# Row maxima of an attention kernel: mask products taken out, one maximum per 64 keys, and a VectorE minimum with a constant table

## The chip, the cores and the metric

The kernel runs on one core of a Trainium2 chip. The metric is the time of one execution on the device in microseconds (us). The engines that matter are TensorE (PE in the profile; PEld are its weight loads), VectorE (DVE), ScalarE (ACT), GpSimd (POOL) and SyncE (SP), which issues nearly all DMAs.

## The reference, cut to what matters

Attention over blocks of 64 positions is followed by a soft mixture of experts and a feed-forward layer. The change concerns the first line on the maximum alone.

```python
# q, k, v: (8, 8, 576, 64); attention of one batch and head:
scores = scale * np.matmul(q, k.transpose(0, 1, 3, 2))
block_i, block_j = pos[:, None] // 64, pos[None, :] // 64
scores = np.where(block_i >= block_j, scores, -1000000000.0)
scores = scores - np.max(scores, axis=-1, keepdims=True)
attn = np.exp(scores)
attn = attn / (np.sum(attn, axis=-1, keepdims=True) + 1e-09)
out = np.matmul(attn, v)
# then, on x = out as (4608, 512): soft mixture of 8 experts, and relu(x @ w_in)**2 @ w_out
```

A query sees all keys of its own block of 64 and of those before it.

## The kernel before, in words

**Stages.** Attention takes the first 430 us or so, the experts come next, and the last third is the feed-forward layer, a dense run of products. The weights of the experts are loaded while attention still runs.

**Attention.** The 64 heads are worked on in 32 pairs: a pair holds one head in each half of a tile, and four pairs make a batch. `pair(n)` writes one turn of a software pipeline: scores and exponentials of pair `n`, values of pair `n - 1`, row maxima of pair `n + 2`, splitting and transposing of pair `n + 3`, and, once in four pairs, the logits and slot weights of a batch that is done (`batch`, whose parts are handed out as `work`). TensorE's order is fixed as it is written; the order of the other engines and of SP's queue is made by a scheduler from dependencies.

**Row maxima.** 576 positions are four units of 128 and a tail of 64. `maxpass(n)` multiplies query units (tile `t`, also called `t1`) by keys (tile `s`, `s1`) into PSUM tiles `ps_max` of 512 columns: `chunk(0)` to `chunk(4)` for the units, and `chunk(5)` and `chunk(6)` for the tails. Each 128 query rows hold two blocks of 64, so in the last 128 keys of a unit the upper 64 rows may not see the second 64 keys. A further product per chunk (`mask`, line 459) adds a huge negative number there: the column tile `mrow_r` of the constant 60000 against the row tile `mrow_l`, which is -60000 for rows 0 to 63 and zero below. VectorE then reduces 512 columns to 4 numbers, one for each 128 keys (`red`, line 465), into tile `pm`, 8 rows of 4 per partition, of which there are two in turn. `fin` reduces `pm` to the row maxima `mx` (lines 498, 499 and 502), writes them as two float16 numbers into tile `qb` (lines 504 and 507), and lets SP transpose `qb` into tile `t2`, also written `t<-qb` (line 512). The second product of `scores` (line 528) subtracts the maximum by means of `t2`.

**Around it on VectorE.** Line 419 makes the low parts of keys (`ka`) and queries (`qb`); `ka` is then transposed by a DMA into `s` (line 426). Lines 364 to 383 work out scales of a pair. Lines 184 to 202 decode the weights `tin`. Lines 761 to 785 are the running maximum of a batch's logits (`mxb`, `mb`, `mrun`, `nm`), and line 816 scales the tokens `x`. On GpSimd, line 571 adds exponentials (`ss`) and line 711 adds the logits of heads (`ul`, `lg`, `ltl`). GpSimd's additions read two tiles in SBUF, as VectorE's lines 507 and 772 do.

Of the kernel before, what the change touches and what calls it, by code (L numbers as in the profile page):

```python
# [8 lines left out]
F32 = mybir.dt.float32  # L9
F32R = mybir.dt.float32r  # L10
F16 = mybir.dt.float16
U32 = mybir.dt.uint32
AF = mybir.ActivationFunctionType
ALU = mybir.AluOpType
# [4 lines left out]
BIG = 60000.0  # L19
# [4 lines left out]
def tile_attn_soft_moe_ffn(  # L24
# [12 lines left out]
    nc = tc.nc  # L37
# [198 lines left out]
    def attention():  # L236
# [13 lines left out]
        mid = st_m.enter_context(tc.tile_pool(name="mid", bufs=1))  # L250
# [10 lines left out]
        NBQ = 3  # L261
        qb = [(even, mid, nat_p)[i].tile([128, NBLK, 128], F16, name=f"qb{i}") for i in range(NBQ)]
        s2 = [pers[i].tile([128, NBLK, 128], F16, name=f"s2_{i}") for i in range(NB2)]
        pm = [mid.tile([128, 8, 4], F32, name=f"pm{i}") for i in range(2)]
        mxs = [mid.tile([128, NBLK], F32, name=f"mx{i}") for i in range(2)]
        junk = mid.tile([128, NBLK, D], mybir.dt.float8e4, name="junk")
        id16 = mid.tile([128, 128], F16, name="id16")
        mrow_l = mid.tile([128, 128], F16, name="mrow_l")
        mrow_r = mid.tile([128, 2], F16, name="mrow_r")

        def prepare():
            nc.vector.tensor_copy(id16, ident)
            for t in qb:
                nc.vector.memset(t, 0.0)
                for i in range(2 * NU):
                    u = i // 2
                    nc.vector.memset(t[0:64, i:i + 1, 66 + u:67 + u], -BIG)
                for h in range(2):
                    nc.vector.memset(t[64 * h:64 * h + 64, 2 * NU:2 * NU + 1, 70 + h:71 + h], -BIG)
            for t in pm:  # L280
                nc.vector.memset(t, -3.0e38)
            nc.vector.memset(mrow_l, 0.0)
            nc.vector.memset(mrow_l[0:1, 0:64], -BIG)
            nc.vector.memset(mrow_r, BIG)
            hi = slice(64, 128)
            a = sm_p.tile([128, 7], F32, tag="sc_a", name="cst")
            nc.vector.tensor_tensor(out=a[hi, 6:7], in0=ident[hi, 64:65], in1=ident[hi, 65:66], op=ALU.add)
            nc.vector.scalar_tensor_tensor(
                out=a[hi, 0:6], in0=ident[hi, 66:72], scalar=BIG / SHIFT, in1=a[hi, 6:7].to_broadcast([64, 6]),
                op0=ALU.mult, op1=ALU.add,  # L290
            )
            for t in s2:
                def put(o, x):
                    nc.vector.tensor_scalar(out=o, in0=x, scalar1=SHIFT, scalar2=None, op0=ALU.mult)

                put(t[hi, 0:8, 0:64], a[hi, 6:7].unsqueeze(2).to_broadcast([64, 2 * NU, 64]))
                for h in range(2):
                    put(t[hi, 8, 64 * h:64 * h + 64], a[hi, 5 - h:6 - h].to_broadcast([64, 64]))
                    put(t[hi, h:8:2, 64:128], a[hi, 0:4].unsqueeze(2).to_broadcast([64, NU, 64]))
# [143 lines left out]
        def maxpass(n):  # L443
            t1, s1 = T[n][0], T[n][1]
            pmt = pm[n % 2]
# [1 line left out]
            ptl = sm_p.tile([128, 5], F32, tag="ptl", name="ptl")  # L447
            mx = mxs[n % 2]

            def part(ps, hp, u, c0):  # L450
                nc.tensor.matmul(  # L451
                    ps[:, c0:c0 + 128 * (u + 1)].rearrange("p (s c) -> p s c", c=128), t1[:, 2 * u + hp, :],
                    s1[:, hp:2 * u + 2:2, :], start=(c0 == 0), stop=False,
                )

            def mask(ps, c0, step, cnt):
                o = ps[:, 0:512].rearrange("p (a x) -> p a x", x=128)
                o = o[:, c0 // 128:c0 // 128 + (cnt - 1) * (step // 128) + 1:max(step // 128, 1), 64:128]
                nc.tensor.matmul(o, mrow_l, mrow_r[:, 0:1].to_broadcast([128, 64 * cnt]), start=False, stop=True)  # L459

            def red(ps, o, w, cnt=None):
                i = ps[:, 0:w].rearrange("p (a x) -> p a x", x=min(128, w))
                if cnt:
                    i = ps[:, 0:w].rearrange("p (c a x) -> p c a x", c=cnt, x=128)
                nc.vector.tensor_reduce(out=o, in_=i, axis=AX.X, op=ALU.max)  # L465

            def chunk(i):
                ps = ps_r.tile([128, 512], F32, tag="r", name="ps_max")
                if i < 2:
                    part(ps, i, 0, 0)  # L470
                    part(ps, i, 2, 128)
                    mask(ps, 0, 384, 2)
                    red(ps, pf[:, 8 * i + 3:8 * i + 7], 512)
                elif i == 2:
                    part(ps, 0, 1, 0)
                    part(ps, 1, 1, 256)
                    mask(ps, 128, 256, 2)
                    red(ps, pmt[:, 4:6, 0:2], 512, 2)
                elif i < 5:
                    part(ps, i - 3, 3, 0)  # L480
                    mask(ps, 384, 128, 1)
                    red(ps, pmt[:, 3 + i, :], 512)
                else:
                    for hp in range(2):
                        h0 = 64 * hp
                        nc.tensor.matmul(
                            ps[h0:h0 + 64, 0:512].rearrange("p (s c) -> p s c", c=128) if i == 5
                            else ps[h0:h0 + 64, 0:64],
                            t1[:, 8, h0:h0 + 64],
                            s1[:, hp:8:2, :] if i == 5 else s1[:, 8, h0:h0 + 64],  # L490
                            start=True, stop=True,
                        )
                    red(ps, ptl[:, 0:4] if i == 5 else ptl[:, 4:5], 512 if i == 5 else 64)

            def fin():
                mv = mx[:, 0:8].rearrange("p (u h) -> p h u", h=2)
                pv4 = pmt.rearrange("p (a b) c -> p a b c", b=2)
                nc.vector.tensor_reduce(out=mv[:, :, 0:3:2], in_=pv4[:, 0:2], axis=AX.X, op=ALU.max)
                nc.vector.tensor_reduce(
                    out=mv[:, :, 1:4:2].rearrange("p h u -> p u h"), in_=pv4[:, 2:4], axis=AX.X, op=ALU.max  # L500
                )
                nc.vector.tensor_reduce(out=mx[:, 8:9], in_=ptl, axis=AX.X, op=ALU.max)
                t = qb[n % NBQ]
                nc.vector.tensor_scalar(
                    out=t[:, :, 64:65], in0=mx.unsqueeze(2), scalar1=-1.0 / SHIFT, scalar2=None, op0=ALU.mult
                )
                nc.vector.scalar_tensor_tensor(
                    out=t[:, :, 65:66], in0=mx.unsqueeze(2), scalar=-1.0 / SHIFT, in1=t[:, :, 64:65],
                    op0=ALU.mult, op1=ALU.subtract,
                )  # L510
                t2 = (mid, odd)[n % 2].tile([128, NBLK, 128], F16, tag="t2", name="t2")
                nc.sync.dma_start_transpose(out=t2, in_=t.rearrange("p s c -> p (s c)"))
                T[n][2] = t2
# [1136 lines left out]
```

## Time and profile before

| what | value |
|---|---|
| median of 3 runs | 893.66 us (890.32 to 896.48) |
| the profiled execution's own time | 893.13 us |
| its span, first to last instruction | 891.3 us |
| TensorE busy | 827.2 us, 93% |
| VectorE busy | 692.7 us, 78% |
| ScalarE busy | 627.5 us, 70% |
| GpSimd busy | 248.3 us, 28% |

The shares are means over stages of different kinds. GpSimd works nearly only in attention. A matmul's busy time includes its way through the pipeline, so two matmuls overlap and a busy TensorE is not one at its peak.

### The profile page before, as it was taken

To read this page: it belongs to the slowest core of one execution; us is meant where nothing else is said; L and a number is where in the kernel's file an instruction comes from. 1 tells how busy PE (TensorE), PEld (TensorE's weight loads), DVE (VectorE), ACT (ScalarE), POOL (GpSimd) and SP (SyncE) were. 2 spreads that over 40 slices of the span, in tenths; PEclk is the share of its full clock that TensorE was granted. 3 is DMA by queue.
4 is the path that set the end of the run, shared out by engine and by line. 5 is a ranking of instruction groups with operands and counts; after the bars stand their busy time and mean duration, and the time that the engine had idled before them with its cause. 6 is when DMAs were issued, how large, how long until landed. Compare 5 with 4: busy or idle time off the path is not lost.

```text
span 891.3 us, 22010 instructions
## 1 busy us (share of the span) xinstructions
PE 827.2 (93%) x8788; PEld 612.9 (69%) x8788; DVE 692.7 (78%) x1600; ACT 627.5 (70%) x1012; POOL 248.3 (28%) x394
## 2 busy tenths in 40 slices
PE   2778999999999989979997799999999999999997
PEld 1446766676666757656532444799998998889996
DVE  5857789989999997953632899888778888888880
ACT  5478787777878786734212789987788888887770
POOL 0234647566665855563100000000000000000000
PEclk9889999999999999999998899999999999999999
DMA  8788899999997797496999500100010000000002
GB/s 168 151 167 159 163 202 174 199 189 198 174 194 157 172 168 172 96 254 194 319 371 371 224 0 1 49 25 25 34 39 25 25 24 25 25 25 24 25 25 48
DMA packets 225191, 113.18 MB, mean 127 GB/s; under 512 B 193856, under 2 KB 202048, under 8 KB 225088
## 3 DMA queue, kind: packets, MB, share of 16 engines
q1 hardware_dynamic: 222432, 111.12, 53.1%
q8 instruction: 69, 1.13, 0.5%
q10 hardware_dynamic: 2656, 0.66, 0.4%
q14 instruction: 34, 0.28, 0.1%
HBM read 78.71 MB, written 9.44 MB: 99 GB/s over the span
## 4 chain that ended last, share of the span: by engine, by line
PE 60%; DVE 9%; DMA 8%; POOL 8%; ACT 8%; SPq 4%; issue 3%; ACTq 0%; DVEq 0%
PE ps_y L1464 14%; PE ps_x L1464 9%; PE ps_z L1464 9%; PE xm L601 5%; POOL ss L571 4%; PE ps_hb L1428 3%; POOL ul L711 3%; DMA s<-ka 3%; PE ps_sc L528 3%; PE po L1486 2%; DMA s<-s 2%; DVE pm L465 2%; PE ps_h L1154 2%; PE ps_max L451 1%; PE tl L612 1%
## 5 line engine op out<-in xcount | busy, mean ns | idle before, releaser
L1464 PEld LDWEIGHTS <-ah 128*128 128x128 f16 x1792 | 170.5, 98 | 21.8 <-issue 0.2
L566 ACT ACTIVATE p<-ps_sc,es 128x512 f32<-128x512 f32 x192 | 128.0, 692 | 40.4 <-PE ps_sc L528 25.9
L1397 DVE TENSOR_TENSOR al<-a,ah 128x1024 f16<-128x1024 f32 (+1 forms) x128 | 138.8, 1127 | 16.9 <-ACT ah L1451 15.5
L571 POOL TENSOR_TENSOR ss<-p 128x384 f32<-128x384 f32 (+1 forms) x128 | 92.8, 746 | 172.7 <-ACT p L566 172.6
L465 DVE TENSOR_REDUCE pm<-ps_max 128x4 f32<-128x512 f32 x160 | 107.4, 683 | 32.1 <-PE ps_max L459 31.8
L1451 ACT CAST ah<-a 128x1024 f16<-128x1024 f32 (+1 forms) x128 | 114.4, 936 | 15.3 <-DVE a L1397 14.0
L528 PE MATMUL ps_sc<-t,s 128*128 128x512 f16 (+3 forms) x512 | 107.7, 304 | 11.4 <-DMA s<-s 7.1
L1557 POOL TENSOR_TENSOR ot<-u,p 128x256 f32<-128x256 f32 x16 | 12.4, 777 | 377.2 <-DVE u L1528 341.5
L1464 PE MATMUL ps_y<-bh,ah 128*128 128x256 f16 x384 | 104.8, 273 | 0.0
L1464 PE MATMUL ps_y<-bl,ah 128*128 128x256 f16 x384 | 104.7, 273 | 0.0
L1464 PE MATMUL ps_y<-bh,al 128*128 128x256 f16 x384 | 104.7, 273 | 0.0
L571 POOL TENSOR_TENSOR ss<-ss,p 128x320 f32<-128x320 f32 (+1 forms) x128 | 98.1, 766 | 10.6 <-ACT p L566 1.5
L1319 ACT ACTIVATE r<-ps_hb,alpha 128x1024 f32<-128x1024 f32 x64 | 71.1, 1112 | 33.9 <-PE ps_hb L1428 33.3
L1464 PEld LDWEIGHTS <-al 128*128 128x128 f16 x896 | 87.7, 98 | 10.0
L601 PE MATMUL xm<-p,ar_hi 128*64 128x256 f32 (+3 forms) x512 | 91.4, 456 | 0.0
L1397 DVE TENSOR_TENSOR a<-a 128x256 f32<-128x256 f32 x192 | 76.2, 425 | 3.9
L1464 PE MATMUL ps_x<-bh,ah 128*128 128x256 f16 x256 | 70.1, 274 | 0.0
L1464 PE MATMUL ps_z<-bh,ah 128*128 128x256 f16 x256 | 69.9, 273 | 0.0
L1464 PE MATMUL ps_x<-bh,al 128*128 128x256 f16 x256 | 69.8, 273 | 0.0
L1464 PE MATMUL ps_z<-bl,ah 128*128 128x256 f16 x256 | 69.8, 273 | 0.0
L1464 PE MATMUL ps_x<-bl,ah 128*128 128x256 f16 x256 | 69.8, 273 | 0.0
L1464 PE MATMUL ps_z<-bh,al 128*128 128x256 f16 x256 | 69.8, 273 | 0.0
(255 smaller groups left out, 1849.7 us busy)
## 6 DMA issues: line engine op xcount, KB each, us to landing
wch<-in_moe_w_dram SPq DMA_DIRECT2D x12, 1024.0 KB, 8.4
ar_hi<-in_v_dram SPq DMA_DIRECT2D x64, 128.0 KB, 3.3
raw<-in_moe_w_in_dram SPq DMA_DIRECT2D x16, 512.0 KB, 5.0
wch<-in_moe_w_dram SPq DMA_DIRECT2D x16, 512.0 KB, 9.0
out_dram<-ot SPq DMA_DIRECT2D x32, 256.0 KB, 2.1
ar_hi<-in_moe_w_dram SPq DMA_DIRECT2D x6, 1024.0 KB, 7.9
s<-s SPq DMA_DIRECT2D x32, 144.0 KB, 3.2
ar_lo<-in_k_dram SPq DMA_DIRECT2D x32, 128.0 KB, 3.1
```

Source lines behind the costliest of these rows:

```text
L465: nc.vector.tensor_reduce(out=o, in_=i, axis=AX.X, op=ALU.max)
L528: nc.tensor.matmul(ps[:, c0:c0 + w].rearrange("p (s c) -> p s c", c=128), kk[:, 2 * t + hp, :], qq[:, 2 * u0 + hp:8:2, :], start=(c0 == 0 ...
L566: exps[:] = [nc.scalar.activation(out=pt, in_=ps, func=AF.Exp, scale=es[:, 0:1])]
L571: add = lambda o, x, y: nc.gpsimd.tensor_tensor(out=o, in0=x, in1=y, op=ALU.add)
L601: nc.tensor.matmul(box["xm"][64 * hp:64 * hp + 64, 128 * t:512], vs[:, t, hp, :], r, start=(t == 0), stop=(t == 3),)
L711: add = lambda o, x, y: nc.gpsimd.tensor_tensor(out=o, in0=x, in1=y, op=ALU.add)
L1154: nc.tensor.matmul(hp_[fh][32 * e4:32 * e4 + 32, :], si[:, dt, s0:s0 + 32], wt[8 * g + KD * fh + dt][e4], start=(dt == 0), stop=(dt == KD ...
L1319: nc.scalar.activation(out=r[:, c0:c1], in_=ps[:, c0:c1], func=AF.Relu, **kw)
L1397: sub = lambda o, a, b: nc.vector.tensor_tensor(out=o, in0=a, in1=b, op=ALU.subtract)
L1428: nc.tensor.matmul(ps[:, 512 * j + 256 * a:512 * j + 256 * a + 256], ws[:, 128 * f:128 * f + 128], ctt[:, c0:c0 + 256], start=True, stop=True,
L1451: nc.scalar.copy(v(hl[n % 2][0][:, 2 * kq:2 * kq + 2], s), v(a7[n, kq], s))
L1464: nc.tensor.matmul(acc[:, 0:HM], a[:, k], b[:, k], start=bool(first and k + j == 0), stop=(k == KH - 1 and j == 2), skip_group_check=not f ...
```

## The change

The mask products and their two constant tiles go. The maximum is taken over 64 keys at a time, so that `red` gives 8 numbers for 512 columns where it gave 4, and `pm` has 8 rows of 8. The forbidden combinations are then single numbers in `pm`. A constant table `cap` (64 partitions of 64 numbers) holds -3e38 at those places and 3e38 elsewhere, and `fin` begins with one VectorE minimum of `pm`'s upper 64 partitions with `cap`, in place. The reductions behind it read 8 numbers where they read 4.

```diff
--- before.py
+++ after.py
@@ -261,12 +261,11 @@
         NBQ = 3
         qb = [(even, mid, nat_p)[i].tile([128, NBLK, 128], F16, name=f"qb{i}") for i in range(NBQ)]
         s2 = [pers[i].tile([128, NBLK, 128], F16, name=f"s2_{i}") for i in range(NB2)]
-        pm = [mid.tile([128, 8, 4], F32, name=f"pm{i}") for i in range(2)]
+        pm = [mid.tile([128, 8, 8], F32, name=f"pm{i}") for i in range(2)]
         mxs = [mid.tile([128, NBLK], F32, name=f"mx{i}") for i in range(2)]
         junk = mid.tile([128, NBLK, D], mybir.dt.float8e4, name="junk")
         id16 = mid.tile([128, 128], F16, name="id16")
-        mrow_l = mid.tile([128, 128], F16, name="mrow_l")
-        mrow_r = mid.tile([128, 2], F16, name="mrow_r")
+        cap = mid.tile([64, 64], F32, name="cap")
 
         def prepare():
             nc.vector.tensor_copy(id16, ident)
@@ -279,9 +278,9 @@
                     nc.vector.memset(t[64 * h:64 * h + 64, 2 * NU:2 * NU + 1, 70 + h:71 + h], -BIG)
             for t in pm:
                 nc.vector.memset(t, -3.0e38)
-            nc.vector.memset(mrow_l, 0.0)
-            nc.vector.memset(mrow_l[0:1, 0:64], -BIG)
-            nc.vector.memset(mrow_r, BIG)
+            nc.vector.memset(cap, 3.0e38)
+            for c0, c1, d in ((7, 24, 16), (13, 30, 16), (35, 44, 8), (55, 64, 8)):
+                nc.vector.memset(cap[:, c0:c1:d], -3.0e38)
             hi = slice(64, 128)
             a = sm_p.tile([128, 7], F32, tag="sc_a", name="cst")
             nc.vector.tensor_tensor(out=a[hi, 6:7], in0=ident[hi, 64:65], in1=ident[hi, 65:66], op=ALU.add)
@@ -447,39 +446,31 @@
             ptl = sm_p.tile([128, 5], F32, tag="ptl", name="ptl")
             mx = mxs[n % 2]
 
-            def part(ps, hp, u, c0):
+            def part(ps, hp, u, c0, last):
                 nc.tensor.matmul(
                     ps[:, c0:c0 + 128 * (u + 1)].rearrange("p (s c) -> p s c", c=128), t1[:, 2 * u + hp, :],
-                    s1[:, hp:2 * u + 2:2, :], start=(c0 == 0), stop=False,
-                )
-
-            def mask(ps, c0, step, cnt):
-                o = ps[:, 0:512].rearrange("p (a x) -> p a x", x=128)
-                o = o[:, c0 // 128:c0 // 128 + (cnt - 1) * (step // 128) + 1:max(step // 128, 1), 64:128]
-                nc.tensor.matmul(o, mrow_l, mrow_r[:, 0:1].to_broadcast([128, 64 * cnt]), start=False, stop=True)
-
-            def red(ps, o, w, cnt=None):
-                i = ps[:, 0:w].rearrange("p (a x) -> p a x", x=min(128, w))
+                    s1[:, hp:2 * u + 2:2, :], start=(c0 == 0), stop=last,
+                )
+
+            def red(ps, o, w, x, cnt=None):
+                i = ps[:, 0:w].rearrange("p (a x) -> p a x", x=x)
                 if cnt:
-                    i = ps[:, 0:w].rearrange("p (c a x) -> p c a x", c=cnt, x=128)
+                    i = ps[:, 0:w].rearrange("p (c a x) -> p c a x", c=cnt, x=x)
                 nc.vector.tensor_reduce(out=o, in_=i, axis=AX.X, op=ALU.max)
 
             def chunk(i):
                 ps = ps_r.tile([128, 512], F32, tag="r", name="ps_max")
                 if i < 2:
-                    part(ps, i, 0, 0)
-                    part(ps, i, 2, 128)
-                    mask(ps, 0, 384, 2)
-                    red(ps, pf[:, 8 * i + 3:8 * i + 7], 512)
+                    part(ps, i, 0, 0, False)
+                    part(ps, i, 2, 128, True)
+                    red(ps, pf[:, 16 * i + 6:16 * i + 14], 512, 64)
                 elif i == 2:
-                    part(ps, 0, 1, 0)
-                    part(ps, 1, 1, 256)
-                    mask(ps, 128, 256, 2)
-                    red(ps, pmt[:, 4:6, 0:2], 512, 2)
+                    part(ps, 0, 1, 0, False)
+                    part(ps, 1, 1, 256, True)
+                    red(ps, pmt[:, 4:6, 0:4], 512, 64, 2)
                 elif i < 5:
-                    part(ps, i - 3, 3, 0)
-                    mask(ps, 384, 128, 1)
-                    red(ps, pmt[:, 3 + i, :], 512)
+                    part(ps, i - 3, 3, 0, True)
+                    red(ps, pmt[:, 3 + i, :], 512, 64)
                 else:
                     for hp in range(2):
                         h0 = 64 * hp
@@ -490,9 +481,10 @@
                             s1[:, hp:8:2, :] if i == 5 else s1[:, 8, h0:h0 + 64],
                             start=True, stop=True,
                         )
-                    red(ps, ptl[:, 0:4] if i == 5 else ptl[:, 4:5], 512 if i == 5 else 64)
+                    red(ps, ptl[:, 0:4] if i == 5 else ptl[:, 4:5], 512 if i == 5 else 64, 128 if i == 5 else 64)
 
             def fin():
+                nc.vector.tensor_tensor(out=pf[0:64], in0=pf[0:64], in1=cap, op=ALU.min)
                 mv = mx[:, 0:8].rearrange("p (u h) -> p h u", h=2)
                 pv4 = pmt.rearrange("p (a b) c -> p a b c", b=2)
                 nc.vector.tensor_reduce(out=mv[:, :, 0:3:2], in_=pv4[:, 0:2], axis=AX.X, op=ALU.max)
```

Lines behind the mask move up by 8 in the new file: its 459 is the old 465, its 487 is the minimum, its 490, 491 and 494 are the old 498, 499 and 502, and its 496 and 499 are the old 504 and 507; 520 is the old 528 and 450 the old 451.

**TensorE, a chunk of two units and one of a single unit.** `ps_max` are products for the maxima, `ps_sc` are scores, `ps_sT` transposes sums. Before:

```order
L451 MATMUL ps_max<-s_2734,t_2733 128x256
L459 LDWEIGHTS mrow_l
L459 MATMUL ps_max<-mrow_r,mrow_l 128x2x64
L528 LDWEIGHTS s_2249
L528 MATMUL ps_sc<-t_2248,s_2249 128x512
L528 LDWEIGHTS s_1_142
L528 MATMUL ps_sc<-t_2684,s_1_142 128x512
L451 LDWEIGHTS t_2733
L451 MATMUL ps_max<-s_2734,t_2733 128x512
L459 LDWEIGHTS mrow_l
L459 MATMUL ps_max<-mrow_r,mrow_l 128x64
L665 MATMUL ps_sT<-ident,sb 128x128 x2
```

After:

```order
L450 MATMUL ps_max<-s_2687,t_2686 128x256
L520 LDWEIGHTS s_2210
L520 MATMUL ps_sc<-t_2209,s_2210 128x512
L520 LDWEIGHTS s_1_142
L520 MATMUL ps_sc<-t_2637,s_1_142 128x512
L450 LDWEIGHTS t_2686
L450 MATMUL ps_max<-s_2687,t_2686 128x512
L657 MATMUL ps_sT<-ident,sb 128x128 x2
```

Each chunk loses its last weight load and product; nothing else on TensorE moves.

**VectorE, the end of the maxima of one pair beside a batch's running maximum.** Before:

```order
L816 TENSOR_TENSOR x<-ps_x,rc 128x4x2x64
L498 TENSOR_REDUCE mx_145<-pm_143 128x2x2
L499 TENSOR_REDUCE mx_145<-pm_143 128x2x2
L190 TENSOR_SCALAR dec_sq<-tin 128x512
L504 TENSOR_SCALAR qb_139<-mx_145 128x9
L771 TENSOR_REDUCE mb<-ps_mx 128x1
L507 SCALAR_TENSOR_TENSOR qb_139<-mx_145,qb_139 128x9
L196 SCALAR_TENSOR_TENSOR dec_sq<-tin,dec_sq 128x512
L772 TENSOR_TENSOR mrun_67<-mrun_66,mb 128x1
L816 TENSOR_TENSOR x<-ps_x,rc 128x4x2x64
L774 TENSOR_SCALAR nm<-mrun_67 128x1
L202 SCALAR_TENSOR_TENSOR tin<-raw,dec_sq 128x512
```

After:

```order
L808 TENSOR_TENSOR x<-ps_x,rc 128x4x2x64
L487 TENSOR_TENSOR pm_143<-pm_143,cap 64x64
L190 TENSOR_SCALAR dec_sq<-tin 128x512
L490 TENSOR_REDUCE mx_145<-pm_143 128x2x2
L491 TENSOR_REDUCE mx_145<-pm_143 128x2x2
L196 SCALAR_TENSOR_TENSOR dec_sq<-tin,dec_sq 128x512
L496 TENSOR_SCALAR qb_139<-mx_145 128x9
L763 TENSOR_REDUCE mb<-ps_mx 128x1
L499 SCALAR_TENSOR_TENSOR qb_139<-mx_145,qb_139 128x9
L202 SCALAR_TENSOR_TENSOR tin<-raw,dec_sq 128x512
L764 TENSOR_TENSOR mrun_67<-mrun_66,mb 128x1
L808 TENSOR_TENSOR x<-ps_x,rc 128x4x2x64
```

The minimum (487) stands in front of the two reductions; the decoding steps 196 and 202 and the pair 504, 507 (now 496, 499) have changed places around it, and nothing else is added in these rows.

**VectorE, the first pair's maxima at the start of the kernel.** Before:

```order
L498 TENSOR_REDUCE mx_145<-pm_143 128x2x2
L502 TENSOR_REDUCE mx_145<-ptl 128x1
L499 TENSOR_REDUCE mx_145<-pm_143 128x2x2
L419 SCALAR_TENSOR_TENSOR qb_140<-ar_lo,sig,qa 128x9x64
L504 TENSOR_SCALAR qb_138<-mx_145 128x9
L465 TENSOR_REDUCE ptl<-ps_max 128x4
L507 SCALAR_TENSOR_TENSOR qb_138<-mx_145,qb_138 128x9
L465 TENSOR_REDUCE ptl<-ps_max 128x1
L465 TENSOR_REDUCE pm_144<-ps_max 128x4 x2
```

After:

```order
L494 TENSOR_REDUCE mx_145<-ptl 128x1
L418 SCALAR_TENSOR_TENSOR qb_140<-ar_lo,sig,qa 128x9x64
L487 TENSOR_TENSOR pm_143<-pm_143,cap 64x64
L459 TENSOR_REDUCE ptl<-ps_max 128x4
L490 TENSOR_REDUCE mx_145<-pm_143 128x2x2
L491 TENSOR_REDUCE mx_145<-pm_143 128x2x2
L459 TENSOR_REDUCE ptl<-ps_max 128x1
L496 TENSOR_SCALAR qb_138<-mx_145 128x9
L459 TENSOR_REDUCE pm_144<-ps_max 128x8
L499 SCALAR_TENSOR_TENSOR qb_138<-mx_145,qb_138 128x9
```

The step that completes `qb` (507, now 499) stands behind one more reduction of 512 columns than before.

## Rows read from the trace of the kernel before

**Rows 1.** Busy time by engine, and VectorE in 40 slices (the page).

```profile
PE 827.2 (93%) x8788; PEld 612.9 (69%) x8788; DVE 692.7 (78%) x1600; ACT 627.5 (70%) x1012; POOL 248.3 (28%) x394
...
DVE  5857789989999997953632899888778888888880
```

**Rows 2.** Busy us (instructions) of PE, PEld, DVE, ACT, POOL; clock, DMA share, GB/s.

```profile
140.00:320.00 180.00, 173.91 (x2444) 124.20 (x2441) 168.74 (x437) 139.38 (x292) 116.99 (x184) 1.00 0.96 182
...
560.00:891.00 331.00, 326.42 (x2936) 291.91 (x2934) 254.84 (x428) 251.29 (x293) 12.44 (x16) 1.00 0.09 30
```

**Rows 3.** Chain of work that ended last, 190 to 222 us: start, length, what.

```profile
192.53 1.28 POOL ss L571 x2
...
204.93 0.75 POOL ltl L711
...
208.35 1.20 DVE pm L465 x2
...
212.24 0.08 DVE mx L498
212.32 0.07 DVE mx L499
...
212.78 0.22 DVE qb L504
...
213.18 0.78 DVE qb L507
...
214.53 0.47 DVE mrun L772
...
217.59 0.73 DVE ka L419
...
218.34 6.24 DMA s<-ka
```

**Rows 4.** Line 459, the mask products: duration ns min/median/max, first and last start, forms.

```profile
L459 PE MATMUL ps_max<-mrow_r,mrow_l x160: 191/219/314, 21.4 to 392.4; 128*128 128x128 f16 x96, 128*128 128x64 f16 x64
```

**Rows 5.** The chain, rows of the mask products: first, a short one, last.

```profile
32.95 0.07 PE ps_max L459
...
315.73 0.03 PE ps_max L459
...
387.47 0.07 PE ps_max L459
```

**Rows 6.** VectorE by shape, 200 to 300 us: busy us, mean ns, idle before.

```profile
L465 DVE TENSOR_REDUCE pm<-ps_max 128x4 f32<-128x512 f32 x41 | 27.5, 680 | 2.8 <-PE ps_max L459 2.8
...
L504 DVE TENSOR_SCALAR qb<-mx 128x9 f16<-128x9 f32 x8 | 4.6, 578 | 0.0
...
L498 DVE TENSOR_REDUCE mx<-pm 128x4 f32<-128x16 f32 x8 | 1.3, 158 | 0.0
...
L772 DVE TENSOR_TENSOR mrun<-mrun,mb 128x1 f32<-128x1 f32 x2 | 1.1, 545 | 0.0
...
L761 DVE TENSOR_REDUCE mxb<-lg 128x32 f32<-128x128 f32 x2 | 0.7, 358 | 0.0
...
L771 DVE TENSOR_REDUCE mb<-ps_mx 128x1 f32<-128x128 f32 x2 | 0.6, 277 | 0.0
...
L762 DVE TENSOR_TENSOR mxb<-mxb,ltl 64x32 f32<-64x32 f32 x2 | 0.4, 184 | 0.3
```

**Rows 7.** The same view from 0 to 100 us.

```profile
L504 DVE TENSOR_SCALAR qb<-mx 128x9 f16<-128x9 f32 x7 | 2.2, 317 | 0.1
```

**Rows 8.** The chain again: the first and the last row of line 498.

```profile
26.03 0.08 DVE mx L498
...
360.20 0.08 DVE mx L498
```

**Rows 9.** Who waited for whom, 100 to 400 us: total, times, longest.

```profile
DVE pm L465 <- PE ps_max L459: 13.5, 22, 2.9
```

**Rows 10.** Idle time before users of tile t, and its cause: us, times.

```profile
  DMA t<-qb: 3.4, 1
```

## The prediction

> **What bounds the kernel now.** I read the page's busy shares first. TensorE is busy for 93% of the span and VectorE for 78%, but VectorE's slices between 111 and 312 us stand at 8 or 9 tenths and more [rows 1]. The change lies in attention alone, so I next asked for busy times by stretch. From 140 to 320 us VectorE is busy for 168.74 of 180 us, TensorE for 173.91, GpSimd for 116.99 (65%) [rows 2]. From 560 us on only products count (326.42 of 331), and nothing there changes. TensorE's share in attention is worth less than it looks, since matmuls overlap; who decides is told by the chain of work that ended last. In each batch of four pairs it goes through GpSimd from 192.53 to 205.7, then through VectorE from about 207.5 to 218.3, then waits for the transposing DMA of the keys, and only then runs on TensorE and ScalarE [rows 3]. So no one engine bounds attention: GpSimd, VectorE, DMA and TensorE take turns. An edit is worth what it changes on the engine whose turn it is.
>
> **Mask products removed.** There are 160, five a pair, 96 of 128 columns and 64 of 64 [rows 4]. In the chain a long one advances the time by 0.06 to 0.07 us and a short one by 0.03 [rows 5]; the weight load before it does not show. All together they are 96 x 0.06 + 64 x 0.03 = 7.7 us of TensorE. On the chain stand 44 of them, the first at 32.95 and the last at 387.47, 2.3 us in all. **Gain: 2.3 us**, between 0 and 7.7.
>
> **The minimum.** It is a new VectorE instruction, 64 partitions by 64 numbers, both inputs in SBUF, once a pair. The nearest row by shape is line 762, the same operation on 64x32: 184 ns, right after GpSimd has finished. With 32 more columns at VectorE's pace (line 465: 512 columns in 680 ns) that is 0.22 us. But line 772, the same operation on one column, takes 545 ns, where a small instruction such as line 498 takes 158 [rows 6]. What sets them apart is GpSimd, which is adding while 772 runs: line 504 likewise averages 578 ns there [rows 6], and 317 at the start, where GpSimd has little to do [rows 7]. So a collision costs about 0.4 us, and with GpSimd busy 65% of the time I take 0.22 + 0.65 x 0.4 = 0.5 us for the minimum; the ends are 0.22 and the 0.8 that line 507 shows in the chain [rows 3].
>
> The Trainium skill has the rule behind this ("SBUF — State Buffer", section "SBUF: two separate sides"): VectorE and GpSimd share a pair of ports as an exclusive lock, which a VectorE operation with two SBUF inputs and a GpSimd operation that reads SBUF take for the whole instruction, the other being fully blocked. It speaks against this change, which buys TensorE time with just such an operation; the trace agrees as far as 545 against 184 ns goes. Without the rule the sum below would end near 893; with it, near 896.
>
> **Wider reductions.** The five reductions of 512 columns write 8 numbers for 4. Line 761 (32 results from 128 columns) takes 358 ns, line 771 (one result) 277 [rows 6]: 31 results cost 81 ns at most, so 4 more cost up to 0.01 us, 0.05 a pair. Two reductions in `fin` read 16 columns more, 0.017 us each. With the minimum a pair costs VectorE 0.50 + 0.05 + 0.03 = 0.58 us more; 32 pairs, 18.6 us.
>
> **What of it lies on the chain.** The end of a pair's maxima is on the chain where line 498 has a row: five times, first at 26.03 and last at 360.20 [rows 8]. The first is at the start with GpSimd idle, 0.25 us; the other four count 0.53 each, 2.1. Three more times only line 504 is on the chain; whether the minimum will be is open, so half, 0.75. The chain has 29 rows of line 465 into `pm` like the one shown [rows 3], 0.01 each, 0.3. **Loss: 3.4 us**, between 1.5 and 6. In the turn that the order shows, the minimum stands between the decoding steps and `mrun`, and the running maximum, two reductions and the keys' low part (line 419) queue behind it; the keys' transposing DMA and TensorE's slot weights wait for those. So it counts in full there.
>
> **GpSimd held up.** A minimum that has begun may make GpSimd wait in turn. No row shows how long; it cannot be more than its own 0.22 us, and in a GpSimd turn of 13 us there is about one (41 reductions into `pm` in 100 us are 8.2 pairs, a pair in 12.2 us). The chain has six such turns, the one shown among them: 0 to 1.3 us. **Loss: 0.6.**
>
> **The rest of the added VectorE time.** 18.6 - 3.4 = 15.2 us fall into stretches where another engine has its turn. VectorE idles for 11.26 us from 140 to 320, 0.76 us a pair, and 0.58 of that would be used up. Much of the idle time is VectorE waiting for the last product of a maximum, 13.5 us in 22 pieces [rows 9], where late work can catch up. I let a tenth through: **loss 1.5 us**, between 0 and all.
>
> **What moves along.** The minimum needs all five reductions, where line 498 could run earlier, so `qb` is complete 0.5 to 1.5 us later in most pairs; behind it in SP's queue stand its transposing DMA, then loads, the copy of `s` and the keys' DMA. A product waited for this transposed tile once, 3.4 us, at the start [rows 10]; elsewhere the tile is needed a pair later, which hides it. At the start one reduction (0.68 us) now stands before the end of the first pair, and two stand behind that of the second pair that stood before: nothing, give or take 1 us. Filling `cap` costs a few small VectorE writes before the first data land.
>
> **Sum,** against the profiled execution's own 893.13 us: 893.1 - 2.3 + 3.4 + 0.6 + 1.5 = 896.3. That execution is within 0.1% of the median of the runs, 893.66, so I predict **896 us**, +0.3%. A measurement of this kernel can tell about 1%, 8.9 us, from no change.
>
> **Rivals.**
>
> First, *VectorE takes over the whole of attention*. Its idle time may not be usable, being made of short waits for TensorE in the middle of a fixed order. Then most of the added 18.6 us counts: with all of it 893.1 - 2.3 + 18.6 = 909.4. It decides from 60% on, 893.1 - 2.3 + 0.6 + 11.2 = 902.6, which is slower by 1%. For it: 93.7% busy from 140 to 320, and 0.18 us of idle left a pair. Against it: in GpSimd's 13 us of each batch, and in the 6.24 us of the keys' DMA [rows 3], VectorE's load sets nothing as long as some idle time is left. Chance 0.20, at about 905.
>
> Second, *TensorE is the bound after all*, being 96.6% busy from 140 to 320, and every mask product counts: 893.1 - 7.7 = 885.4, with VectorE's part in idle time but for a few tenths, 886. Against it: the chain has only 44 of the 160 products, and between them are turns of other engines of 10 us and more. Chance 0.10, of which half beyond 1% if the new order of the queues helps too.
>
> Third, *the minimum meets GpSimd seldom* and costs 0.22 us: 893.1 - 2.3 + 1.5 + 0.3 = 892.6. Chance 0.15; it lies within 1%.
>
> **How the numbers follow.** The forecast, 896 with 892 to 901 of its own, has 0.55. Faster by over 1% (under 884.7) is only the far half of the second rival and luck in the order: 0.06. Slower by over 1% (over 902.6) is the first rival: 0.20. The rest, 0.74, is within 1%. The range of 8 in 10 reaches down to the second rival's 886 and up into the first rival, 907.
>
> **What would show it.** In the profile after: no line 459 as a product; 32 minima averaging 0.4 to 0.6 us between 140 and 320 and near 0.2 at the start, which tells the collision from its absence; the 512-column reductions still near 0.68 us; VectorE above 96% busy from 140 to 320; the same turns in the chain, with the minimum in VectorE's. I am wrong on the slow side if the chain's GpSimd and DMA turns shrink and VectorE fills them, and on the fast side if VectorE's waits for products get shorter without the stage's other turns getting longer.

## The result and the profile after

The changed kernel takes **899.46 us** (median of 20 runs, 895.07 to 903.85) beside 893.18 us for the kernel before (20 runs, 888.88 to 898.69). The ratio is 1.0071, 95% interval 1.0057 to 1.0086: 6.3 us slower, within the 1% that I had set as no change. I had said 896. Slower was right and the size was half of it, and the experiments show that the terms of my sum did not make it up as I thought.

The profiled execution took 899.5 us. Line numbers of the changed kernel: products of the maxima 450 (before 451), reductions into `pm` 459 (465), the minimum 487, `fin`'s reductions 490, 491 and 494 (498, 499, 502), the two halves of the maximum in `qb` 496 and 499 (504 and 507), `mrun` 764 (772). The page, as in [rows 1]: busy time, and VectorE's 40 slices.

```profile
PE 821.3 (92%) x8628; PEld 608.1 (68%) x8628; DVE 696.0 (78%) x1634; ACT 627.5 (70%) x1012; POOL 250.9 (28%) x394
...
DVE  5867788999899999972551899888877888888880
```

TensorE has 6 us less to do, as it should without 160 products. VectorE has 3.3 us more, where I had added 18.6. Busy time by stretch, columns as in [rows 2]:

```profile
140.00:320.00 180.00, 168.42 (x2271) 118.89 (x2263) 165.47 (x433) 136.52 (x281) 117.89 (x183) 0.98 0.93 183
560.00:897.00 337.00, 333.05 (x2952) 294.77 (x2950) 261.45 (x436) 258.06 (x299) 13.52 (x16) 1.00 0.08 29
```

From 140 to 320 us VectorE is busy for less time than before, 165.47 us against 168.74. That fall alone proves little: kernels without a minimum have 165.10 (experiment 7) and 169.76 (experiment 3) in the same stretch. But the 0.58 us a pair that I had added do not show either, and why is seen in VectorE by shape from 200 to 300 us, which answers to [rows 6]:

```profile
L459 DVE TENSOR_REDUCE pm<-ps_max 128x8 f32<-128x512 f32 x42 | 28.1, 678 | 4.4 <-PE ps_max L450 4.4
...
L487 DVE TENSOR_TENSOR pm<-pm,cap 64x64 f32<-64x64 f32 x8 | 2.9, 364 | 0.0
...
L496 DVE TENSOR_SCALAR qb<-mx 128x9 f16<-128x9 f32 x8 | 1.6, 205 | 0.0
L499 DVE SCALAR_TENSOR_TENSOR qb<-mx,qb 128x9 f16<-128x9 f32 x8 | 1.5, 184 | 0.0
L490 DVE TENSOR_REDUCE mx<-pm 128x4 f32<-128x32 f32 x8 | 1.4, 174 | 0.0
...
L764 DVE TENSOR_TENSOR mrun<-mrun,mb 128x1 f32<-128x1 f32 x2 | 0.3, 148 | 0.0
```

The minimum costs 364 ns, near what I had taken. But line 504, which took 578 ns before, takes 205 ns as line 496, and `mrun` 148 instead of 545. The collision with GpSimd was not added. It moved to the instruction that now comes first. This holds over the whole kernel. The minimum and the two lines of `qb`, all 32 pairs:

```profile
L487 DVE TENSOR_TENSOR pm<-pm,cap 64x64 f32<-64x64 f32 x32 | 12.4, 388 | 0.1
...
L496 DVE TENSOR_SCALAR qb<-mx 128x9 f16<-128x9 f32 x32 | 7.9, 247 | 0.0
...
L499 DVE SCALAR_TENSOR_TENSOR qb<-mx,qb 128x9 f16<-128x9 f32 x32 | 7.1, 222 | 0.0
```

The kernel of experiment 8 is the changed one without the minimum, and there the two lines take their waits back:

```profile
L498 DVE SCALAR_TENSOR_TENSOR qb<-mx,qb 128x9 f16<-128x9 f32 x32 | 13.3, 415 | 0.1
L495 DVE TENSOR_SCALAR qb<-mx 128x9 f16<-128x9 f32 x32 | 12.3, 384 | 0.1
```

With `mrun` (1.9 and 3.2 us) that is 29.3 us with the minimum and 28.8 without. The wider reductions are as expected, 678 ns into `pm`, and 174 for `fin`'s, where it was 158.

The chain of work that ended last still takes its turns as in [rows 3], GpSimd, VectorE, DMA of the keys, TensorE:

```profile
212.71 0.77 POOL lg L703
...
219.88 0.60 DVE pm L459
220.48 0.91 DVE tin L184
221.39 0.60 DVE x L808
221.99 0.60 DVE pm L487
222.59 0.33 DVE dec_sq L190
222.93 0.10 DVE mx L490
...
223.93 0.10 DVE qb L496
224.03 0.18 DVE mb L763
224.20 0.11 DVE qb L499
...
224.88 0.07 DVE mrun L764
...
229.03 5.95 DMA s<-ka
234.98 0.05 issue
235.03 0.39 PE ps_max L450 x2
```

The minimum stands where the prediction put it, between the decoding and `mrun`, with 0.60 us. Lines 496, 499 and 764 behind it take 0.28 us together, where lines 504, 507 and 772 took 1.47.

One more place differs, at the very start. The chain there, after:

```profile
11.04 0.17 DVE sc_a L363
11.23 0.16 DVE cst L287
11.39 1.92 DVE s L293 x10
13.32 0.18 DVE sc_h L366
```

And the kernel before, where `sc_h` follows `sc_a` at once, the constants having been written while the first data were on the way:

```profile
11.05 0.17 DVE sc_a L364
11.25 0.18 DVE sc_h L367
```

The scheduler, with five writes of `cap` to place, put `sc_a`, which waits for TensorE until 11.04, ahead of ten constant writes (line 293) and the small addition before them (line 287). These now run behind that wait, and the first queries and keys wait for them: 2.07 us.

**Theories.** *The start*: the loss is this delay and what follows from it in the first 90 us, where the changed kernel's trace is 7.3 us behind the old one's by the fifth pair (its scores' line 538, 546 before, starts at 96.7 us, before at 89.5). *The minimum*: its collisions and its length cost time in every pair. The prediction's *mask term* has to be checked too, 2.3 us gained.

### The profile page after: what moved, and what is told of

The parts are those of the page before. It is cut to its first block, busy times and chain, and to the rows that moved or that the text cites. A ratio compares the mean times of both kernels' runs of the same rounds, so it can differ in the third digit from the quotient of the medians.

```text
span 897.6 us, 21713 instructions
## 1 busy us (share of the span) xinstructions
PE 821.3 (92%) x8628; PEld 608.1 (68%) x8628; DVE 696.0 (78%) x1634; ACT 627.5 (70%) x1012; POOL 250.9 (28%) x394
## 4 chain that ended last, share of the span: by engine, by line
PE 63%; DVE 10%; DMA 8%; ACT 7%; POOL 7%; issue 3%; SPq 1%; ACTq 0%; DVEq 0%
PE ps_y L1456 14%; PE ps_x L1456 9%; PE ps_z L1456 9%; PE xm L593 6%; PE ps_sc L520 3%; PE ps_hb L1420 3%; POOL ss L563 3%; POOL ul L703 3%; DVE pm L459 2%; PE po L1478 2%; DMA s<-s 2%; DMA s<-ka 2%; PE ps_h L1146 2%; PE ps_max L450 2%; PE tl L604 1%
## 5 line engine op out<-in xcount | busy, mean ns | idle before, releaser
L459 DVE TENSOR_REDUCE pm<-ps_max 128x8 f32<-128x512 f32 x160 | 107.4, 681 | 36.1 <-PE ps_max L450 35.5
L593 PE MATMUL xm<-p,ar_hi 128*64 128x256 f32 (+3 forms) x512 | 93.4, 464 | 0.0
L450 PE MATMUL ps_max<-s,t 128*128 128x128 f16 (+3 forms) x256 | 63.5, 317 | 9.1 <-DMA s<-ka 5.5
```

Of the source, the lines that this page charges most:

```text
L450: nc.tensor.matmul(ps[:, c0:c0 + 128 * (u + 1)].rearrange("p (s c) -> p s c", c=128), t1[:, 2 * u + hp, :], s1[:, hp:2 * u + 2:2, :], star ...
L593: nc.tensor.matmul(box["xm"][64 * hp:64 * hp + 64, 128 * t:512], vs[:, t, hp, :], r, start=(t == 0), stop=(t == 3),)
```

## The experiments

Ratios are to runs of the kernel before on the same chip. For a difference of two ratios the interval is the root of the sum of the squares of both.

**1. The table's writes later.** Five writes moved behind the constants.

```diff
             for t in pm:
                 nc.vector.memset(t, -3.0e38)
-            nc.vector.memset(cap, 3.0e38)
-            for c0, c1, d in ((7, 24, 16), (13, 30, 16), (35, 44, 8), (55, 64, 8)):
-                nc.vector.memset(cap[:, c0:c1:d], -3.0e38)
...
+            nc.vector.memset(cap, 3.0e38)
+            for c0, c1, d in ((7, 24, 16), (13, 30, 16), (35, 44, 8), (55, 64, 8)):
+                nc.vector.memset(cap[:, c0:c1:d], -3.0e38)
```

> The changed kernel with one thing moved: the five writes that fill the table cap stand at the end of prepare(), behind the small constants. Nothing is computed differently. Theory of the start (the loss is made in the first 90 us, because the constants fell behind the wait for the first score row of PE): the first transpose of a key tile is issued about 2 us earlier, at some 13.7 instead of 15.8 us, and the time is 897.4 us (899.5 - 2.1); if the later waits on the SP queue at pairs 2 to 4 hang on this start too, down to 892. Rival, the minimum's price in the steady stretch: the start gets its 2 us back, but the time stays within 1 us of 899.5.

Measured: 899.69 us, ratio 1.0071 (1.0043 to 1.0100). The start is mended, as its chain shows:

```profile
11.34 0.17 DVE sc_a L363
11.53 0.18 DVE sc_h L366
```

The time is not: 0.0 us against the changed kernel, give or take 2.9. A gain of 2.1 us is not excluded, the 892 is. The fifth pair still starts 5.9 us later than in the kernel before, at 95.4 us. So the rest of the early lag does not hang on the start.

**2. The table alone, in the kernel before.**

```diff
+        cap = mid.tile([64, 64], F32, name="cap")
...
+            nc.vector.memset(cap, 3.0e38)
+            for c0, c1, d in ((7, 24, 16), (13, 30, 16), (35, 44, 8), (55, 64, 8)):
+                nc.vector.memset(cap[:, c0:c1:d], -3.0e38)
```

> The kernel before, with only the table cap and its five writes added in place; the table is read by nothing, and masks, maxima and reductions are the old ones. Theory of the start: the same constants fall behind the same wait, so the first transpose comes 2 us later, and the time is 895.3 us or more (893.2 + 2.1), without any minimum. Rival, the minimum's price: five writes of some 60 ns each at the start, 893.2 to 893.7.

Measured: 895.54 us, ratio 1.0015 (0.9995 to 1.0035), 1.3 us, give or take 1.8. The chain has the same ten constants behind `sc_a` as the changed kernel. This fits the 2.1 us of the start and does not exclude nothing at all.

**3. No minimum and no table.** Everything else of the change stays.

```diff
-        cap = mid.tile([64, 64], F32, name="cap")
...
-            nc.vector.memset(cap, 3.0e38)
-            for c0, c1, d in ((7, 24, 16), (13, 30, 16), (35, 44, 8), (55, 64, 8)):
-                nc.vector.memset(cap[:, c0:c1:d], -3.0e38)
...
-                nc.vector.tensor_tensor(out=pf[0:64], in0=pf[0:64], in1=cap, op=ALU.min)
```

> The changed kernel without the minimum and its table, so that the maxima take in the masked keys too (that part of the computation is left out); the mask products stay out and the maxima stay one per 64 keys. Theory of the start: the start order is that of the kernel before, so 2 us come back at once; the five collisions that the minimum took over from the later VectorE instructions go back to those (the reductions L496 and L499 at about 0.58 and 0.37 us instead of 0.21 and 0.18), so the steady stretch gains little: 892 to 895. Rival, the minimum's price: all of the 6.3 us and the 2.3 us of the mask products come back, 890 to 891.

Measured: 895.18 us, ratio 0.9999 (0.9974 to 1.0024). The loss is in the minimum and its table, to within 2.2 us. The rival's 2.3 us on top did not show; the interval just reaches them, and experiment 7 settles them. The expected move of the waits came: lines 491 and 494, `fin`'s two of `qb`, take 391 and 351 ns in the mean, where 496 and 499 took 247 and 222.

**4. The forbidden places written over.** Three writes of a constant stand in for the minimum; no table.

```diff
-                nc.vector.tensor_tensor(out=pf[0:64], in0=pf[0:64], in1=cap, op=ALU.min)
+                nc.vector.memset(pf[0:64, 7:39].rearrange("p (i x) -> p i x", x=16)[:, :, 0:7:6], -3.0e38)
+                for c0 in (35, 55):
+                    nc.vector.memset(pf[0:64, c0:c0 + 9:8], -3.0e38)
```

> The changed kernel with the minimum replaced by three writes of -3e38 onto the places of the maxima that the mask forbids; no table, and so no writes of it at the start. The result is the same. Theory of the start: the start order is that of the kernel before and the pair has no instruction with two SBUF sources ahead of the reductions, so 892 to 896, and the wait for GpSimd shows at L496 and L499 again. Rival, the minimum's price is one of instructions and dependencies on VectorE: three small writes of some 0.06 to 0.2 us cost as much as one minimum of 0.39, so 898 to 900.

Measured: 892.96 us, ratio 0.9977 (0.9955 to 1.0000), 8.4 us below the changed kernel, give or take 2.4. Three instructions on the same data at the same point cost nothing that shows. The waits of `qb`'s lines came back in part, 251 and 358 ns in the mean. Its trace also shows what the early lag is worth. SP's queue has a wait at the transposition of `qb` between 60 and 95 us, which I had taken for a cause of the loss: 4.0 us in the changed kernel, 1.5 in the kernel before. In the changed kernel, what SP waits for there:

```profile
SPq L504 <- DVE qb L499: 4.0, 1, 4.0
```

And with the places written over:

```profile
SPq L502 <- DVE qb L497: 4.3, 1, 4.3
```

The wait is as long, and the kernel is not slower. TensorE's granted clock falls to half, 1.2 GHz, at about the same time in both: its mean from 85 to 90 us is 0.66 in the one and 0.69 in the other, after products had waited 3.3 and 3.7 us for the copy of `s`. So neither the queue nor the clock there explains the 6 us, as far as one trace of each can tell. The lag by the fifth pair is 5.4 us in this trace and 4.4 in that of experiment 7, which both end level with the kernel before: it is mostly the one trace of before that was early there.

**5. The minimum made small, and with one source.** First over 2 columns, in an order that on SP is that of experiment 3 but for 4 rows of 496:

```diff
-                nc.vector.tensor_tensor(out=pf[0:64], in0=pf[0:64], in1=cap, op=ALU.min)
+                nc.vector.tensor_tensor(out=pf[0:64, 7:9], in0=pf[0:64, 7:9], in1=cap[:, 7:9], op=ALU.min)
```

> The changed kernel with the minimum cut to 2 of the 64 columns (7 and 8), so that most masked keys stay in the maxima (that part of the computation is left out). It keeps one instruction with two SBUF sources ahead of the reductions in each pair, but its order on SP and VectorE is that of the kernel without a minimum but for a few rows. Theory of collisions (what costs is that an instruction with two SBUF sources meets GpSimd's sums): the price stays, 898 to 900, and L487 is seen waiting at 0.3 us or more in the mean. Theory of order and length (what costs is that the full minimum puts the rows of the two queues in another order and stands before the reductions with its 0.2 us): 894 to 896, the time without a minimum.

Then over all 64, against a number:

```diff
-                nc.vector.tensor_tensor(out=pf[0:64], in0=pf[0:64], in1=cap, op=ALU.min)
+                nc.vector.tensor_scalar(out=pf[0:64], in0=pf[0:64], scalar1=3.0e38, scalar2=None, op0=ALU.min)
```

> The changed kernel with the minimum taken against the number 3e38 in place of the table: the same 64 columns, the same place, but one SBUF source (the masked keys stay in the maxima, that part is left out). The order on SP differs from that of the changed kernel in 16 rows of 496. Theory of collisions: a one-source instruction as short as the reductions beside it does not wait for GpSimd, so 894 to 896, with L496 and L499 waiting again. Theory of order and length: 898 to 900.

Measured: 900.96 us, ratio 1.0093 (1.0061 to 1.0125), and 899.68 us, ratio 1.0085 (1.0053 to 1.0118). The price stays with a thirty-second of the columns and another order; it stays with one source too. Collision and order each failed one half of the test as I had written it: the small minimum speaks against order and length, and the one-source minimum was to have no collision by the first theory, but has one (below). The small minimum also missed the mean of 0.3 us that the collision theory gave it, and left the waits where they had been:

```profile
L499 DVE SCALAR_TENSOR_TENSOR qb<-mx,qb 128x9 f16<-128x9 f32 x32 | 13.6, 426 | 0.0
...
L496 DVE TENSOR_SCALAR qb<-mx 128x9 f16<-128x9 f32 x32 | 11.9, 373 | 0.1
...
L487 DVE TENSOR_TENSOR pm<-pm,cap 64x2 f32<-64x2 f32 x32 | 7.1, 221 | 0.0
```

Whether the minimum or the lines behind it take the waits made no difference to the time that shows. Both kernels keep the table, which neither theory had priced, and this led to experiments 8 and 9.

**6. The minimum twice.** The line is repeated.

```diff
                 nc.vector.tensor_tensor(out=pf[0:64], in0=pf[0:64], in1=cap, op=ALU.min)
+                nc.vector.tensor_tensor(out=pf[0:64], in0=pf[0:64], in1=cap, op=ALU.min)
```

> The changed kernel with the minimum issued twice in a row (the second changes nothing). If each minimum has its price of some 6.3 us (collision or length), 905 to 906. If the first takes the collision and the second costs only its unhindered 0.2 us, 32 times 0.2 us at most: 899.5 to 906, with the second at 0.21 us in the mean. If the price is that of the order alone, within 2 us of 899.5.

Measured: 901.26 us, ratio 1.0091 (1.0062 to 1.0119), 1.8 us above the changed kernel, give or take 2.9. That a second minimum costs another 6.3 us is excluded. It was not unhindered either: its mean is 415 ns where 0.21 us was expected, and that of the first is 355. VectorE is busy for 704.5 us, 8.5 more than in the changed kernel, so at least some 4 us of its added time did not lengthen the run.

**7. No mask products, in the kernel before.** Nothing stands in for them; the product ahead of each closes its sum.

```diff
-                    mask(ps, 0, 384, 2)
...
-                    mask(ps, 128, 256, 2)
...
-                    mask(ps, 384, 128, 1)
```

> The kernel before with the 160 mask products left out and nothing put in their place (the masked keys stay in the maxima; that part is left out). By the forecast's term, 44 of them lie on the chain with 2.3 us: 891 (ratio 0.9975). Rival, they lie in time in which TensorE waits anyway: 893 to 894, ratio 0.999 to 1.001. Beside the kernel without a minimum at 0.9999 this also prices the wider reductions alone: 0.6 us by the forecast.

Measured: 893.53 us, ratio 1.0006 (0.9987 to 1.0025): +0.5 us, give or take 1.7. **Taking 160 products out gains nothing that shows**, and the 2.3 us of the forecast are excluded. Where the time goes instead is not shown. The obvious candidate is the keys' transposing DMA, for which the first products of the maxima wait (line 451 in both kernels). TensorE's waits for it (us in total, times, the longest), kernel before:

```profile
PE ps_max L451 <- DMA s<-ka: 5.6, 5, 2.0
```

Without mask products:

```profile
PE ps_max L451 <- DMA s<-ka: 7.4, 6, 2.3
```

That looks like an answer, but other kernels speak against it. That of experiment 3 has no mask products either, and waits less:

```profile
PE ps_max L446 <- DMA s<-ka: 4.6, 3, 2.2
```

That of experiment 2 has all of them and waits 8.0 us, in 6 pieces. So this wait differs from trace to trace by more than the 1.8 us in question, with the products or without; and on the chain this DMA has four turns in the kernel before and four without the products, 22.7 us in both. VectorE is busy in this kernel for 165.10 us from 140 to 320, with no minimum in it, as much as in the changed kernel: a share in one stretch of one trace does not tell these kernels apart.

**8. The table without the minimum.** Table and writes stay.

```diff
-                nc.vector.tensor_tensor(out=pf[0:64], in0=pf[0:64], in1=cap, op=ALU.min)
```

> The changed kernel with its table cap and the five writes of it, but without the minimum (the masked keys stay in the maxima; that part is left out). Its order is that of the kernel without table and minimum but for 7 rows of VectorE. Theory of the instruction (an instruction on the maxima ahead of the reductions that is no plain write or reduction costs the time, whatever its size): 894 to 896, ratio 0.999 to 1.003, since there is none. Rival, the table (its place in SBUF moves what lies behind it, its writes delay the start): 898 to 901, ratio 1.005 to 1.009.

Measured: 898.66 us, ratio 1.0043 (1.0020 to 1.0067). Beside experiment 3 the table costs 3.9 us, give or take 3.1, and beside this run the minimum costs 2.5 us, give or take 2.5. The measured value lies between what the two theories gave, and its interval reaches both. What it shows is that the table has a price without a minimum. What is left for the minimum is at the edge of the noise. The kernels of experiments 5 and 6 lie 3.7 to 4.5 us above this one, give or take 3.3 to 3.6, so that something does seem to be left; but all of these are taken against the one measurement here. The order of SP's queue is, row for row, that of experiment 3, so the table's price is not in that order.

**9. The one-source minimum without the table.**

```diff
-        cap = mid.tile([64, 64], F32, name="cap")
...
-            nc.vector.memset(cap, 3.0e38)
-            for c0, c1, d in ((7, 24, 16), (13, 30, 16), (35, 44, 8), (55, 64, 8)):
-                nc.vector.memset(cap[:, c0:c1:d], -3.0e38)
```

> The one-source minimum again, now without the table and its writes (the masked keys stay in the maxima; that part is left out); the order on SP is the same as with them. Theory of the instruction: 898 to 901, ratio 1.005 to 1.009, as with the table. Rival, the table: 893 to 896.

Measured: 897.93 us, ratio 1.0022 (0.9998 to 1.0045). It lies between the two expectations: 2.1 us above no minimum (give or take 3.1), 5.6 us below the same with the table (give or take 3.6).

**10. The minimum behind the transposition.** Same instruction, moved to the end of `fin`.

```diff
                 nc.sync.dma_start_transpose(out=t2, in_=t.rearrange("p s c -> p (s c)"))
                 T[n][2] = t2
+                nc.vector.tensor_tensor(out=pf[0:64], in0=pf[0:64], in1=cap, op=ALU.min)
```

> The changed kernel with the same minimum issued at the end of the maximum pass, behind the transposition of the small rows, where nothing needs its result any more (the masked keys stay in the maxima; that part is left out). Theory of the path (the minimum costs because the reductions, the small rows and their transposition stand behind it): 894 to 896. Rival, GpSimd and VectorE collide 32 times more often wherever the instruction stands: 898 to 901. Rival, the table: 898 to 901 too, and then the run with the table and no minimum tells.

Measured: 900.36 us, ratio 1.0050 (1.0027 to 1.0074). By the run with the table and no minimum (1.0043) it costs 0.7 parts in a thousand, 0.6 us, give or take 3.0. Whether it costs less there than in its own place (2.5 ± 2.5) is not told apart.

**11. Two writes instead of three.** The edit is against experiment 4.

```diff
-                for c0 in (35, 55):
-                    nc.vector.memset(pf[0:64, c0:c0 + 9:8], -3.0e38)
+                nc.vector.memset(pf[0:64, 24:64].rearrange("p (i x) -> p i x", x=20)[:, :, 11:20:8], -3.0e38)
```

> The kernel with the forbidden places written over, with two writes of 64 x 4 instead of three (the result is the same as the reference's). If the writes of 0.06 us are as good as free, the time is that of three writes, 892 to 894, ratio 0.996 to 1.000; if each instruction ahead of the reductions has a price, it gains up to 2 us on that.

Measured: 895.20 us, ratio 0.9991 (0.9969 to 1.0014). The writes are free to within what can be told. Neither version with writes is told from the kernel before; both are faster than the changed kernel.

## Why the prediction was right, and where it was not

Four of these kernels lead in steps from before to after, so their differences add up to the whole:

| step | us |
|---|---|
| mask products out (experiment 7) | +0.5 ± 1.7 |
| reductions to 64 keys (3 against 7) | -0.6 ± 2.8 |
| table and its writes (8 against 3) | +3.9 ± 3.1 |
| minimum (after against 8) | +2.5 ± 2.5 |

The forecast of 896 was on the right side and inside its range, but in part by luck: the gain from the mask products and the price of the table were each off by 2 us or more, two losses were counted for which nothing was found, and the minimum's mechanism was not what the trace shows.

**Mask products removed: this step failed.** The sum took 2.3 us because 44 of them stood on the chain with that much time. They did stand there, yet without them the kernel took 0.5 us more, give or take 1.7. I had asked of no row what would be late next, and which wait took their place stays open: the traces do not agree on it (experiment 7).

**The minimum on the chain: the size fits, the mechanism does not.** 3.4 us forecast, 1.5 to 6; measured 2.5 ± 2.5. The collision is real and near the size that I had read from [rows 6]: on the chain 0.60 us, by shape 364 ns, and 388 in the mean of all 32. But I had added it to a chain that otherwise stayed, and in the turn shown the minimum and lines 496, 499 and 764 take 0.88 us together where 504, 507 and 772 took 1.47. On that turn the chain became 0.6 us shorter. So that the size fits is luck as far as is known, and how the minimum costs what it costs is not shown; experiment 10 could not tell. That it would be near 0.2 us at the start was wrong. From 0 to 100 us:

```profile
L487 DVE TENSOR_TENSOR pm<-pm,cap 64x64 f32<-64x64 f32 x7 | 2.9, 417 | 0.1
```

**The added VectorE time was mis-sized**: 18.6 us in the sum, 3.3 in the trace, because I took the minimum's wait as new where it took over the waits of the lines behind it. So VectorE did not come above 96% from 140 to 320 (165.47 of 180 us, 92%), and the first rival, that VectorE takes over, has fallen; experiment 6 speaks against it too, where 8.5 us more of VectorE cost 1.8 ± 2.9. The term of 1.5 us for the rest, and the 0.6 for GpSimd held up, cannot be told apart from zero here.

**"What moves along" failed.** I had priced the table at a few writes "before the first data land", at nothing. It pushed ten constant writes behind a wait (2.07 us in the trace). Three runs price the table: 1.3 ± 1.8, 3.9 ± 3.1 and 5.6 ± 3.6. A price of about 2.5 us is in all three intervals, and that of the start would nearly do; but mending the start alone gained 0.0 ± 2.9. Whether the table costs anything beyond the start, by its place in SBUF or by VectorE's order around it, stays open. The other half of that step, the transposition of `qb` and the queue behind it, was right to be priced at nothing: a wait of 4.3 us there cost nothing that shows in experiment 4.

**The other rivals.** That TensorE is the bound fell with experiment 7. That the minimum seldom meets GpSimd fell too: 25 of 32 do (last section).

**The sum mended.** Without the 2.3 us that were not gained, and with some 2.5 us for the table, it would be 896.3 + 2.3 + 2.5 = 901.1; without the 0.6 and the 1.5 for which nothing was found, 899.0, beside 899.46 measured. So errors of both signs cancelled in part, and the 3 us that were missing can be made up of the mask products and the table, less these two. This is a fit after the fact: each of its terms is known to 2 or 3 us only.

## What to carry to other kernels

An instruction's time on the chain is no forecast of what its removal gains: 2.3 us on the chain brought nothing here, so look for what would be late next before you count. A wait that grows in one trace is no cause yet: look for it in a kernel that lacks the change. When two engines collide, a new instruction in front of others that already collide can take over their waits, so price the group of them and not the new one alone. A table of constants need not be free: here it cost 3.9 ± 3.1 us, part of it perhaps because a scheduler placed its writes so that others fell behind the first wait of the kernel. Writing the constant straight into the data cost nothing that shows.

## What the runs showed of the hardware

Which VectorE instructions wait for GpSimd was sharper than I had expected. Durations in ns, least, median and most, then first and last start and shape: the minimum after, and `fin`'s first reduction:

```profile
L487 DVE TENSOR_TENSOR pm<-pm,cap x32: 205/274/1066, 28.8 to 402.0; 64x64 f32<-64x64 f32 x32
```

```profile
L490 DVE TENSOR_REDUCE mx<-pm x32: 167/174/189, 29.5 to 403.0; 128x4 f32<-128x32 f32 x32
```

The minimum over two columns (experiment 5), and with one source and no table (9):

```profile
L487 DVE TENSOR_TENSOR pm<-pm,cap x32: 142/147/997, 28.0 to 391.5; 64x2 f32<-64x2 f32 x32
```

```profile
L483 DVE TENSOR_SCALAR pm<-pm x32: 175/240/650, 26.8 to 398.8; 64x64 f32<-64x64 f32 x32
```

A write of a constant into the same tile (4):

```profile
L485 DVE MEMSET pm<- x64: 60/60/60, 26.3 to 400.6; 64x2 f32 x64
```

Reductions and constant writes did not wait, though 28 of these 32 reductions and 50 of these 64 writes overlapped an instruction of GpSimd. Minima did, those over two numbers and those with one source too. Matched with GpSimd's own rows, the seven minima of the changed kernel that meet no GpSimd instruction take 206 to 216 ns, and the 25 that meet one 205 to 1066. That one VectorE source suffices is also what line 504 had shown (578 ns, [rows 6]). The Trainium skill ("SBUF — State Buffer", section "SBUF: two separate sides") names operations with two SBUF inputs or in a two-port mode as those that take the lock; in which mode the one-source minimum ran, no run here shows.
